# Where a recurrence's carry is computed: TensorE order, and work handed from VectorE to ScalarE and GpSimd

## The chip, the core and the metric

The kernel runs on one core of one Trainium2 chip. The metric is the device time of one execution in microseconds (us). Before the change it is 202.56 us, the median of three executions (202.4, 202.56 and 202.63). The profile was taken in an execution of 202.6 us; from its first to its last instruction it spans 200.9 us, and every start time below counts from that first instruction.

The engines are named as the profile names them: PE is TensorE's matmuls, PEld its weight loads, DVE is VectorE, ACT is ScalarE, POOL is GpSimd, SP is SyncE, which only issues transfers here. A transpose on TensorE is a matmul against the identity and shows as MATMUL.

## What is computed

Two blocks stand one behind the other. The first is a linear recurrence with decay, for 4 batches, 8 heads, 768 steps and heads 48 wide:

```python
for t in range(S):
    cur = np.einsum('bhd,bhe->bhde', u[None] * kt, vt)
    y[:, :, t] = np.einsum('bhd,bhde->bhe', rt, state + cur)
    state = wt[:, :, :, None] * state + np.einsum('bhd,bhe->bhde', kt, vt)
```

Its output, laid out as 4 batches of 768 rows of 384 numbers, is `x` of the second block, a mixture of depths: in each batch the 128 rows with the highest scores go through a two-layer network and are added back, all other rows are passed through.

```python
scores = np.einsum('bsd,d->bs', x, w_gate)
top_idx = np.argpartition(-scores[b], capacity)[:capacity]      # 128 of 768
h = np.maximum(x[b, top_idx] @ w1, 0.0);  ye = h @ w2           # 384 -> 1024 -> 384
out[b, top_idx] = x[b, top_idx] + sigmoid(scores[b, top_idx])[:, None] * ye
```

## The kernel before

The 768 steps of a batch are cut into 6 chunks of 128, so there are 24 chunks, numbered n = 0 to 23 through all batches. Inside a chunk the recurrence becomes matrix products, with k and r scaled by running products of the decay (`K`, `R`); from chunk to chunk a state of 48x48 per head is carried. The last chunk of a batch (n = 5, 11, 17, 23) hands nothing on.

The kernel is written as a loop of turns, and each engine runs its instructions in the order in which the turn lists them. Turn i does the main work of chunk i, prepares chunks i+1 and i+2, and finishes chunk i-1; the network's matmuls are fed in between in small pieces (`fed_in_turn`) as soon as a batch's rows are picked.

```python
def turn(i):
    step(first_left, i + 1)                       # ACT, one column
    ...
    step(own_products, i + 1)                     # POOL  r*k
    step(scores, i)                               # PE    16 matmuls into ps_s
    step(own_values, i)                           # ACT   8 heads, each with a sum
    step(carry, i - 1, work.get(i))               # DVE and POOL: next state
    if i > 0:
        step(scaled, i + 1, "K", "right")         # DVE
    if i >= 0:
        step(own_weights, i + 1)                  # POOL  times u
    ...
    if i < N:
        step(compared, i - 2)                     # PE ps_e, DVE ahead, ACT every
    step(back, i)                                 # PE 4 transposes, ACT copies them to kt
    mix(place="half")
    if not soon:
        step(masked, i)                           # DVE   sc <- ps_s * mask
    step(rows_out, i - 1, soon)                   # PE ps_y, ACT x, POOL x + vo, DMA out
    step(row_scores_soon if soon else row_products, i - 1)   # POOL scr
    step(own_results, i)                          # POOL  vo = v * own
    fed_in_turn(PIECES // 2, 2 if i >= N - 1 else 1)         # PE pieces of the network
    step(inputs_t, i + 1, "R", r_bufs)            # PE 4 transposes
    ...
    step(scaled, i + 1, "R", "left")              # DVE
    step(decays_t, i + 2)                         # PE 4 transposes into ps_w
    mix(place="mid")
    ...
    step(range_check, i + 2)                      # ACT
    ...
    step(outputs_t, i)                            # PE ps_yt, ACT copies it to yt
    step(carry_products, i)                       # PE ps_kv
    fed_in_turn(PIECES - PIECES // 2, 1 if i == N - 1 else 0)
    ...
    step(inputs_t, i + 2, "K", k_bufs)            # PE 4 transposes
    ...
    if not soon:
        step(row_sums, i - 1)                     # ACT
    step(scans, i + 2)                            # DVE, two scans over ps_w
    ...                                           # mix(place="end"), loads
```

The steps that the change or the argument touches, cut:

```python
def own_values(t):
    ...
    for h in range(H):
        nc.scalar.activation(out=rk[:, h, :], in_=rk[:, h, :], func=AF.Copy,
                             accum_out=o[:, h:h + 1])

def outputs_t(t):
    old = state.get(n)
    ps = psS.tile([L, 2, HP, L], FP32, tag="s", name="ps_yt")
    ...   # 16 matmuls of vt and sc, and 16 more of old and R where there is a state
    t["yt"] = lev.tile([L, 2, HP // 2, L], FP32, tag="yt", name="yt")
    nc.scalar.copy(out=t["yt"], in_=ps[:, :, 0:HP // 2, :])

def back(t):
    ...
    ps = dense(psT, "t", lambda j: t["K"][0:DE, j, :], lambda j: 0)
    t["kt"] = kt_bufs[t["n"] % 2]
    nc.scalar.copy(out=t["kt"][:, :, :, 0:D], in_=ps...)

def carry_products(t):
    ...
    t["kv"] = kv = psK.tile([L, HP, D], FP32, tag="kv", name="ps_kv")
    ...   # 16 matmuls of t["kt"] and v

def compared(t):
    ...
    ps = psW.tile([L, L], FP32, tag="w", name="ps_e")
    nc.tensor.transpose(ps, own.to_broadcast([L, L]), ident)
    ...   # DVE: L508 (chunks 1 to 5 of a batch) and L512
    if ci < NCH - 1:
        nc.scalar.copy(out=every[:, lo:hi], in_=ps)
```

Three PSUM pools with one buffer each matter. `psS` holds `ps_s` (the scores) and `ps_yt` (the outputs) in turn, so the scores of the next chunk can only be written when ScalarE has copied `ps_yt` away. `psW` holds `ps_w` (the transposed decays) and `ps_e` (the transposed scores of rows) in turn. `psK` holds `ps_kv`.

Of the kernel before, what the change touches and what calls it, by code (L numbers as in the profile page):

```python
# [10 lines left out]
FP32 = mybir.dt.float32  # L11
# [3 lines left out]
AF = mybir.ActivationFunctionType  # L15
# [3 lines left out]
L = 128  # L19
DP = 64  # L20
NBUF = 4
# [16 lines left out]
def kernel(  # L38
# [40 lines left out]
    nc = tc.nc  # L79
    PSUM = bass.MemoryType.PSUM  # L80

    B, H, S, D = r.shape
# [2 lines left out]
    CAP = moe_capacity  # L85
    NCH = S // L
    HP = H // 2
    NDC = C // L
    NFC = F // L
    NHF = NCH // 2  # L90
    W = HP * L
    DE = DP + D
    assert S % (2 * L) == 0 and C % L == 0 and F % (4 * L) == 0 and H % 2 == 0
    assert HP % 2 == 0 and D <= DP and W <= 512 and C <= 512 and 0 < CAP < S and CAP % L != 1
    assert B * NCH < 256
# [3 lines left out]
    lev = ctx.enter_context(tc.tile_pool(name="lev", bufs=2))  # L99
# [17 lines left out]
    def half(q):  # L117
        return slice(DP * q, DP * q + DP)
# [5 lines left out]
    v_bufs = [consts.tile([L, H, DP], FP32, name=f"v_buf{i}") for i in range(NBUF)]  # L124

    for queue, hs in ((nc.sync, slice(H // 2, H)), (nc.scalar, slice(0, H // 2))):
        queue.dma_start(
            out=w_bufs[0][:, hs, 0:D], in_=w[0, hs, 0:L, :].rearrange("h t d -> t h d")
# [22 lines left out]
    def loads(n):  # L151
        load(v_bufs, v, n - 3)
        load(k_bufs, k, n - 1)
        load(r_bufs, r, n - 1)
        load(w_bufs, w, n)


    for bufs, x, n in (
# [4 lines left out]
    loads(3)  # L163
    w1 = consts.tile([L, NDC, F], FP32)
    w2 = consts.tile([L, NFC, C], FP32)


    weights = [
        (w1[:, i, :], moe_w1[i * L:(i + 1) * L, :]) for i in range(NDC)
    ] + [  # L170
# [25 lines left out]
    for x in (0, 1):  # L196
        for to, src in ((0, DP * x), (D, DP * (1 - x)), (2 * D, D)):
            n = min(D, DE - to)
            nc.gpsimd.tensor_copy(out=turned[:, x, to:to + n], in_=ident[0:DE, src:src + n])
    kt_bufs = [consts.tile([L, HP, 2, DP], FP32, name=f"kt{i}") for i in range(2)]  # L200
    for t in kt_bufs:
# [9 lines left out]
    for t, sign in ((before_f, 1), (after_f, -1)):  # L211
        nc.gpsimd.memset(t, 1.0)
        nc.gpsimd.affine_select(
            out=t, in_=t, pattern=[[sign, L]], base=-1, channel_multiplier=-sign,
# [17 lines left out]

    from_right = consts.tile([L, HP, L], FP32)
    nc.vector.memset(from_right, 0.0)
    nc.vector.memset(from_right[:, :, L - 1], 1.0)
    from_left = [consts.tile([L, HP, L], FP32, name=f"from_left{i}") for i in range(2)]
    for t, fill in zip(from_left, (nc.vector, nc.gpsimd)):
        fill.memset(t, 0.0)
    right_bufs = [consts.tile([L, HP, L], FP32, name=f"right_buf{i}") for i in range(3)]
    for t in right_bufs:  # L240
# [6 lines left out]
    def warm(n):  # L247

        ps = psM.tile([L, 512], FP32, tag="m", name="ps_n")
        for _ in range(n):  # L250
            nc.tensor.matmul(ps, nothing[:, 0:L], nothing, start=True, stop=True)

    def spread(to, row):

        ps = psM.tile([L, C], FP32, tag="m", name="ps_b")
        nc.tensor.matmul(ps, one_row, row, start=True, stop=True)
        nc.scalar.copy(out=to, in_=ps)
# [46 lines left out]
    def check_sums():  # L304

        above = setup.tile([L, 1], FP32)
        nc.vector.tensor_reduce(out=above, in_=guard, axis=AX.X, op=ALU.add)
        below = setup.tile([L, 1], FP32)
        junk = setup.tile([L, N * HP], FP32)
        nc.vector.tensor_scalar(  # L310
            out=junk, in0=alls.rearrange("p n j -> p (n j)"), scalar1=float(LOW ** L),
            scalar2=None, op0=ALU.is_lt, op1=ALU.add, accum_out=below,
        )
        return above, below
# [49 lines left out]
            )  # L364

    def own_results(t):
        t["vo"] = lev.tile([L, H, D], FP32, tag="vo", name="vo", bufs=3)
        nc.gpsimd.tensor_mul(  # L368
            t["vo"], v_bufs[t["n"] % NBUF][:, :, 0:D], t.pop("own").to_broadcast([L, H, D])
        )  # L370

    def scores(t):
        t["ps_s"] = ps = psS.tile([L, 2, HP, L], FP32, tag="s", name="ps_s")
        for j in range(HP):
            for q in (0, 1):
                rows = slice(DP * q, DP * q + D)
                nc.tensor.matmul(  # L377
                    ps[:, q, j, :], t["K"][rows, j, :], t["R"][rows, j, :],
                    start=True, stop=True,
                )  # L380
# [16 lines left out]
    state = {}  # L397
# [60 lines left out]
    def carry_products(t):  # L458
        n = t["n"]
        if chunks[n][1] == NCH - 1:  # L460
            return
        t["kv"] = kv = psK.tile([L, HP, D], FP32, tag="kv", name="ps_kv")
        for j in range(HP):
            for q in (0, 1):
                nc.tensor.matmul(  # L465
                    kv[half(q), j, :], t["kt"][:, j, q, :],
                    v_bufs[n % NBUF][:, 2 * j + q, 0:D], start=True, stop=True,
                )

    def carry(t, nxt):  # L470

        n = t["n"]
        if "kv" not in t:
            return
        kv = t.pop("kv")
        by = nxt["all"].to_broadcast([L, HP, D])
        new = state[n + 1] = lev.tile([L, HP, D], FP32, tag="state", name="state")
        if n in state:
            mid = lev.tile([L, HP, D], FP32, tag="mid", name="mid")
            nc.vector.tensor_add(mid, kv, state[n])  # L480
            nc.gpsimd.tensor_mul(new, mid, by)
        else:
            nc.vector.tensor_mul(new, kv, by)


    groups = [(c0, min(L, CAP - c0)) for c0 in range(0, CAP, L)]
# [32 lines left out]
    def mixture(b):  # L519
# [21 lines left out]
        for gi, (c0, n) in enumerate(groups):  # L541
# [35 lines left out]

            ps = psT.tile([L, NDC, L], FP32, tag="t", name="ps_x")
            for dc in range(NDC):
                nc.tensor.transpose(ps[:, dc, :], xe[:, dc * L:(dc + 1) * L], ident)  # L580
            xeT = mod.tile([L, NDC, L], FP32, name="xeT", bufs=2)
            nc.scalar.copy(out=xeT, in_=ps)  # L582
# [20 lines left out]
    def forward(b, n, idx, xe, xeT, gate, gated):  # L603
# [6 lines left out]
        for f0 in range(0, NFC, 4):  # L610
# [3 lines left out]
            for q in range(4):  # L614
                for dc in range(NDC):
                    nc.tensor.matmul(  # L616
# [33 lines left out]
    def step(f, n, *more):  # L650
        if 0 <= n < N:
            f(work.setdefault(n, dict(n=n)), *more)

    def mix(n=1, place=None):


        while n > 0 and mixing:
            if place is not None and mixing[0][1] not in (None, place):
                return
            try:  # L660
                mixing[0][1] = next(mixing[0][0])
                n -= 1
            except StopIteration:
                mixing.pop(0)
# [16 lines left out]
    def fed_in_turn(n, few):  # L681

        kept = (feed or picked) and (feed or picked)[0][0] == B - 2
        fed(few if kept else n, on=False)
# [6 lines left out]
    def turn(i):  # L691
        soon = i >= N - 1
        step(first_left, i + 1)
        if i < 1:
            step(scaled_aside, i + 1, "K", "right")
        step(own_products, i + 1)
        step(scores, i)
        step(own_values, i)
        step(carry, i - 1, work.get(i))
        if i > 0:  # L700
            step(scaled, i + 1, "K", "right")
        if i >= 0:
            step(own_weights, i + 1)
        if soon:
            step(masked, i)
        if i == N - 1:
            sums.extend(check_sums())
        if i < N:
            step(compared, i - 2)
        step(back, i)  # L710
        mix(place="half")
        if not soon:
            step(masked, i)
        step(rows_out, i - 1, soon)
        step(row_scores_soon if soon else row_products, i - 1)
        step(own_results, i)
        fed_in_turn(PIECES // 2, 2 if i >= N - 1 else 1)
        step(inputs_t, i + 1, "R", r_bufs)
        if i == -1:
            spread(wg_bc, wg_row)  # L720
        step(scaled, i + 1, "R", "left")
        step(decays_t, i + 2)
        mix(place="mid")
        if i == -2:
            warm(2)
        step(range_check, i + 2)
        if i == -1:
            spread(u_bc.rearrange("p h d -> p (h d)"), u_row)
            step(own_weights, i + 1)
        step(outputs_t, i)  # L730
        step(carry_products, i)
        fed_in_turn(PIECES - PIECES // 2, 1 if i == N - 1 else 0)
        if i == N - 1:
            step(compared, i - 1)
        step(inputs_t, i + 2, "K", k_bufs)
        if i == -2:
            warm(1)
        if not soon:
            step(row_sums, i - 1)
        step(scans, i + 2)  # L740
        if 0 <= i - 2 < N - 1 and chunks[i - 2][1] == NCH - 1:
            mixing.append([mixture(chunks[i - 2][0]), "end"])
        mix(place="end")
        if i > -2:
            loads(i + 5)
        if i in WEIGHT_TURNS:
            load_weights(1)
# [93 lines left out]
```

## Time and profile before

| quantity | value |
|---|---|
| median time | 202.56 us |
| span of the profiled execution | 200.9 us |
| busy: PE / PEld | 188.8 us (94%) / 152.9 us (76%) |
| busy: DVE | 160.9 us (80%) |
| busy: ACT | 120.7 us (60%) |
| busy: POOL | 136.6 us (68%) |
| granted TensorE clock | 0.994 |
| `mid` on DVE (L480) | 16 instructions, mean 340 ns |
| first state of a batch on DVE (L483) | 4 instructions, mean 332 ns |
| `state` on POOL (L481) | 16 instructions, mean 506 ns |
| `vo` on POOL (L368) | 24 instructions, mean 830 ns |

The busy times are averages over a program with two very different stages, so they do not say what bounds it; the strip of 40 slices, each 5.02 us wide, does that better. A timeline line gives the start, the length, the engine, the program line, and what was written from what. On VectorE and ScalarE the next instruction often starts before the listed end of the one before, so the cost of an instruction to its engine is read from start to start, not from its length. An idle time stands in square brackets with the instruction that the profile holds to have ended it. The profile names the releaser that came last by its own clock; where the engine named had long been done, another one was meant.

### The profile page before, as it was taken

What the parts mean: (1) busy time and instruction counts of PE and PEld (TensorE: products, weight loads), DVE (VectorE), ACT (ScalarE), POOL (GpSimd) and SP (SyncE); (2) the same over time, 40 slices, a digit from 0 to 9 for tenths busy, and PEclk for the clock granted to TensorE, in tenths of its full rate; (3) what the DMA queues carried; (4) which work ended last, traced back from release to release, by engine and by line L of the source; (5) the groups of instructions that cost most, each with busy time, mean ns of one, the idle gap of its engine ahead of it and who ended that gap; (6) DMA issues with size and microseconds to landing.
All of it is one profiled execution on the core that took longest, in us unless ns stands there. A gap on an engine that the chain in (4) does not pass through costs nothing.

```text
span 200.9 us, 6399 instructions
## 1 busy us (share of the span) xinstructions
PE 188.8 (94%) x2289; PEld 152.9 (76%) x2289; DVE 160.9 (80%) x355; ACT 120.7 (60%) x619; POOL 136.6 (68%) x175
## 2 busy tenths in 40 slices
PE   7899999989799999999999999999999999999970
PEld 2487888767687898897877898897877898866830
DVE  7899999999999968989978888989978884951010
ACT  5586887768754865787456675787456676410300
POOL 8498789886859997669639798668639797121201
PEclk9999999999999999999999999999999999999997
DMA  7999999999989999899894794897764031111101
GB/s 117 163 163 166 178 180 197 223 212 231 197 138 268 251 192 192 209 236 173 175 137 106 136 210 104 128 172 146 139 98 109 17 111 44 39 44 41 39 8 44
DMA packets 105387, 28.81 MB, mean 143 GB/s; under 512 B 100482, under 2 KB 104580, under 8 KB 105348
## 3 DMA queue, kind: packets, MB, share of 16 engines
q1 hardware_dynamic: 104304, 26.65, 74.7%
q0 software_dynamic: 512, 1.57, 2.7%
q8 instruction: 20, 0.33, 0.7%
q14 instruction: 19, 0.16, 0.3%
q10 hardware_dynamic: 532, 0.10, 0.2%
HBM read 22.81 MB, written 5.51 MB: 141 GB/s over the span
## 4 chain that ended last, share of the span: by engine, by line
PE 76%; DVE 9%; ACT 2%; issue 1%; POOL 0%; POOLq 0%; DVEq 0%; ACTq 0%
PE ps_h L616 11%; PE ps_f L628 11%; PE ps_s L377 10%; PE ps_yt L410 10%; PE ps_t L263 8%; PE ps_yt L418 5%; PE ps_kv L465 4%; PE ps_w L263 4%; PE ps_y L270 4%; PE ps_t L270 3%; PE ps_e L506 3%; DVE left L294 2%; DVE right_buf L283 2%; DVE sc L385 1%; DVE R L341 1%
## 5 line engine op out<-in xcount | busy, mean ns | idle before, releaser
L362 ACT ACTIVATE rk<-rk 128x48 f32<-128x48 f32 x192 | 43.7, 230 | 0.1
L435 POOL TENSOR_TENSOR x<-x,vo 128x384 f32<-128x384 f32 x22 | 22.1, 1004 | 22.0 <-ACT x L434 21.9
L362 ACT ACTIVATION_READ_ACCUMULATOR rk<-rk 128x1 f32 x192 | 36.2, 189 | 0.0
L423 ACT COPY yt<-ps_yt 128x512 f32<-128x512 f32 x24 | 14.1, 585 | 29.6 <-PE ps_yt L418 27.3
L294 DVE TENSOR_TENSOR_SCAN left<-ps_w,from_left 128x511 f32<-128x511 f32 x24 | 30.7, 1280 | 0.9
L385 DVE TENSOR_TENSOR sc<-ps_s,before_f 128x1024 f32<-128x1024 f32 x24 | 29.2, 1218 | 0.8 <-PE ps_s L377 0.8
L283 DVE TENSOR_TENSOR_SCAN right_buf<-ps_w,from_right 128x511 f32<-128x511 f32 x24 | 29.1, 1211 | 0.7 <-PE ps_w L263 0.7
L377 PE MATMUL ps_s<-R,K 48*128 48x128 f32 x384 | 27.9, 285 | 0.3 <-ACT yt L423 0.2
L410 PE MATMUL ps_yt<-sc,v_buf 128*64 128x128 f32 x384 | 26.3, 278 | 2.0 <-PE ps_w L263 1.6
L377 PEld LDWEIGHTS ps_s<-R,K 48*128 48x128 f32 x384 | 23.3, 187 | 3.9 <-issue 3.2
L616 PE MATMUL ps_h<-xeT,w 128*128 128x128 f32 x192 | 25.6, 280 | 0.2 <-ACT hid L621 0.2
L410 PEld LDWEIGHTS ps_yt<-sc,v_buf 128*64 128x64 f32 x384 | 20.7, 136 | 6.4 <-PE ps_w L263 2.9
L356 POOL TENSOR_TENSOR rk<-rk,u_bc 128x384 f32<-128x384 f32 x24 | 24.0, 1002 | 1.6 <-DVE alls L289 0.9
L353 POOL TENSOR_TENSOR rk<-r_buf,k_buf 128x384 f32<-128x384 f32 x24 | 24.2, 1007 | 0.0
L616 PEld LDWEIGHTS ps_h<-xeT,w 128*128 128x128 f32 x192 | 22.9, 192 | 1.6 <-ACT xeT L582 0.5
L628 PE MATMUL ps_f<-w,hid 128*128 128x384 f32 x64 | 23.8, 500 | 0.0
L440 POOL TENSOR_TENSOR scr<-x,wg_bc 128x384 f32<-128x384 f32 x22 | 22.0, 1000 | 1.7
L368 POOL TENSOR_TENSOR vo<-v_buf,own 128x384 f32<-128x384 f32 x24 | 19.9, 830 | 1.3 <-ACT rk L362 1.3
L341 DVE TENSOR_TENSOR R<-ps_t,left 128x512 f32<-128x512 f32 x24 | 16.4, 685 | 3.3 <-ACT own L594 1.3
L341 DVE TENSOR_TENSOR K<-ps_t,right_buf 128x512 f32<-128x512 f32 x22 | 15.1, 684 | 4.6 <-PE ps_t L263 4.6
L263 PE MATMUL ps_w<-ident,w_buf 128*128 128x128 f32 x96 | 15.0, 279 | 1.0 <-ACT every L517 0.7
L263 PE MATMUL ps_t<-ident,k_buf 128*128 128x128 f32 x96 | 15.0, 279 | 0.4 <-DMA k_buf<-in_k_dram 0.4
(111 smaller groups left out, 341.8 us busy)
## 6 DMA issues: line engine op xcount, KB each, us to landing
k_buf<-in_k_dram SPq DMA_DIRECT2D x24, 192.0 KB, 5.3
r_buf<-in_r_dram SPq DMA_DIRECT2D x24, 192.0 KB, 5.3
v_buf<-in_v_dram SPq DMA_DIRECT2D x24, 192.0 KB, 4.6
out_dram<-x SPq DMA_DIRECT2D x24, 192.0 KB, 2.4
w_buf<-in_w_dram SPq DMA_DIRECT2D x23, 192.0 KB, 4.7
w<-in_moe_w_dram SPq DMA_DIRECT2D x3, 512.0 KB, 5.9
w<-in_moe_w_dram SPq DMA_DIRECT2D x4, 384.0 KB, 4.9
w_buf<-in_w_dram ACTq DMA_DIRECT2D x1, 96.0 KB, 3.2
```

The source lines that it names most:

```text
L263: nc.tensor.transpose(ps[:, j, :], src(j), ident)
L283: nc.vector.tensor_tensor_scan(out=flat[:, W - 2::-1], data0=wt[:, W - 1:0:-1], data1=from_right.rearrange("p j t -> p (j t)")[:, W - 2::- ...
L294: nc.vector.tensor_tensor_scan(out=left.rearrange("p j t -> p (j t)")[:, 1:W], data0=wt[:, 0:W - 1], data1=start.rearrange("p j t -> p (j ...
L341: nc.vector.tensor_mul(out, t.pop(name + "t"), t.pop(by))
L353: nc.gpsimd.tensor_mul(rk, r_bufs[n % NBUF][:, :, 0:D], k_bufs[n % NBUF][:, :, 0:D])
L356: nc.gpsimd.tensor_mul(t["rk"], t["rk"], u_bc)
L362: nc.scalar.activation(out=rk[:, h, :], in_=rk[:, h, :], func=AF.Copy, accum_out=o[:, h:h + 1])
L377: nc.tensor.matmul(ps[:, q, j, :], t["K"][rows, j, :], t["R"][rows, j, :], start=True, stop=True,)
L385: nc.vector.tensor_mul(t["sc"].rearrange("p q j t -> p (q j) t"), ps.rearrange("p q j t -> p (q j) t"), _heads(before_f, 2 * HP),)
L410: nc.tensor.matmul(ps[half(c), j % 2, j // 2, :], vt[:, 2 * j + q, :], t["sc"][:, q, j, :], start=(j < 2), stop=(old is None), skip_group_ ...
L616: nc.tensor.matmul(ps[:, q, :], w1[:, dc, (f0 + q) * L:(f0 + q + 1) * L], xeT[:, dc, :], start=(dc == 0), stop=(dc == NDC - 1),)
L628: nc.tensor.matmul(ps, hid[:, fc, :], w2[:, fc, :], start=(fc == 0), stop=(fc == NFC - 1))
```

## The change

The change does three things. **First**, in every turn the carry's products (`ps_kv`, TensorE) are put in front of the chunk's outputs (`ps_yt`) instead of behind them. **Second**, for chunks with n < 9 (`AHEAD = S // L + 3`) ScalarE copies `ps_kv` from PSUM to an SBUF tile at once, and the sum with the old state, or for the first chunk of a batch the product that makes the first state, is done by GpSimd from that copy instead of by VectorE from PSUM. **Third**, for chunks 1 to 8 half of the heads of `vo` are computed by ScalarE, one instruction a head with a per-row scale, and GpSimd does the other half, as a balance for what it got. Its purpose is to take work off VectorE in the stretch before the network's matmuls begin.

```diff
--- before.py
+++ after.py
@@ -85,6 +85,8 @@
     CAP = moe_capacity
     NCH = S // L
     HP = H // 2
+
+    AHEAD = S // L + 3
     NDC = C // L
     NFC = F // L
     NHF = NCH // 2
@@ -364,10 +366,17 @@
             )
 
     def own_results(t):
-        t["vo"] = lev.tile([L, H, D], FP32, tag="vo", name="vo", bufs=3)
+        n, own = t["n"], t.pop("own")
+        vo = t["vo"] = lev.tile([L, H, D], FP32, tag="vo", name="vo", bufs=3)
+        vt = v_bufs[n % NBUF]
+        some = H // 2 if 0 < n < AHEAD else H
         nc.gpsimd.tensor_mul(
-            t["vo"], v_bufs[t["n"] % NBUF][:, :, 0:D], t.pop("own").to_broadcast([L, H, D])
-        )
+            vo[:, 0:some, :], vt[:, 0:some, 0:D], own[:, 0:some].to_broadcast([L, some, D])
+        )
+        for h in range(some, H):
+            nc.scalar.activation(
+                out=vo[:, h, :], in_=vt[:, h, 0:D], func=AF.Copy, scale=own[:, h:h + 1]
+            )
 
     def scores(t):
         t["ps_s"] = ps = psS.tile([L, 2, HP, L], FP32, tag="s", name="ps_s")
@@ -466,6 +475,9 @@
                     kv[half(q), j, :], t["kt"][:, j, q, :],
                     v_bufs[n % NBUF][:, 2 * j + q, 0:D], start=True, stop=True,
                 )
+        if n < AHEAD:
+            t["kv"] = lev.tile([L, HP, D], FP32, tag="kvs", name="kvs")
+            nc.scalar.copy(out=t["kv"], in_=kv)
 
     def carry(t, nxt):
 
@@ -475,12 +487,13 @@
         kv = t.pop("kv")
         by = nxt["all"].to_broadcast([L, HP, D])
         new = state[n + 1] = lev.tile([L, HP, D], FP32, tag="state", name="state")
+        aside = n < AHEAD
         if n in state:
             mid = lev.tile([L, HP, D], FP32, tag="mid", name="mid")
-            nc.vector.tensor_add(mid, kv, state[n])
+            (nc.gpsimd if aside else nc.vector).tensor_add(mid, kv, state[n])
             nc.gpsimd.tensor_mul(new, mid, by)
         else:
-            nc.vector.tensor_mul(new, kv, by)
+            (nc.gpsimd if aside else nc.vector).tensor_mul(new, kv, by)
 
 
     groups = [(c0, min(L, CAP - c0)) for c0 in range(0, CAP, L)]
@@ -727,8 +740,8 @@
         if i == -1:
             spread(u_bc.rearrange("p h d -> p (h d)"), u_row)
             step(own_weights, i + 1)
+        step(carry_products, i)
         step(outputs_t, i)
-        step(carry_products, i)
         fed_in_turn(PIECES - PIECES // 2, 1 if i == N - 1 else 0)
         if i == N - 1:
             step(compared, i - 1)
```

## The prediction

> **What bounds the kernel now.** I read the strip of slices first, because the shares of the whole span hide the stages. Its lines for PE and DVE:
>
> ```profile
> PE   7899999989799999999999999999999999999970
> DVE  7899999999999968989978888989978884951010
> ```
>
> From slice 2 to slice 14, roughly 10 to 70 us, VectorE is full. From 70 us on TensorE is full (10.00 of 10 us busy in each window from 70 to 160 us, when the windows are asked for) and VectorE has gaps. The first stage is turns 0 to 9; there the change removes its work. Next I read the timeline of VectorE in turn 4:
>
> ```profile
> 33.34 0.33 DVE L480 TENSOR_TENSOR mid<-ps_kv,state 128x192 f32<-128x192 f32 x1
> 33.59 0.68 DVE L341 TENSOR_TENSOR K<-ps_t,right_buf 128x512 f32<-128x512 f32 x1
> 34.18 0.47 DVE L508 TENSOR_SCALAR_CACHE_REDUCE ahead<-every,score 128x256 bf16<-128x256 f32 x1
> ...
> 34.85 1.22 DVE L385 TENSOR_TENSOR sc<-ps_s,before_f 128x1024 f32<-128x1024 f32 x1
> 35.99 0.68 DVE L341 TENSOR_TENSOR R<-ps_t,left 128x512 f32<-128x512 f32 x1
> 36.58 1.21 DVE L283 TENSOR_TENSOR_SCAN right_buf<-ps_w,from_right 128x511 f32<-128x511 f32 x1
> ```
>
> No line has an idle time in brackets. `mid` is listed with 0.33 us, but `K` starts 0.25 us after it: **0.25 us** is what taking it away can give. The starts of `R` in turns 1 to 9 (18.12, 23.92, 29.88, 35.99, 42.22, 48.33, 54.83, 62.10, 68.07) give turns of 5.80, 5.96, 6.11, 6.23, 6.11, 6.50, 7.27 and 5.97 us. They grow because L508 compares with ever more columns; turn 8 holds the picking of 128 rows.
>
> TensorE has little room in the same stage. Turn 2 to 3:
>
> ```profile
> 25.12 0.65 PE L418 MATMUL ps_yt<-R,state 64*48 64x128 f32 x16
> 25.71 0.67 PE L465 MATMUL ps_kv<-v_buf,kt 128*64 128x48 f32 x16
> 26.31 0.66 PE L263 MATMUL ps_t<-ident,k_buf 128*128 128x128 f32 x4
> 26.90 1.16 PE L377 MATMUL ps_s<-R,K 48*128 48x128 f32 x16
> ...
> 29.36 0.60 PE L263 MATMUL ps_w<-ident,w_buf 128*128 128x128 f32 x4
> 30.07 1.09 PE L410 MATMUL ps_yt<-sc,v_buf 128*64 128x128 f32 x16
> ```
>
> and ScalarE beside it:
>
> ```profile
> 25.90 0.59 ACT L423 COPY yt<-ps_yt 128x512 f32<-128x512 f32 x1 [1.37 <-PE ps_yt L418]
> 26.38 0.53 ACT L445 ACTIVATE scr<-scr 128x384 f32<-128x384 f32 x1
> ...
> 28.57 0.23 ACT L362 ACTIVATE rk<-rk 128x48 f32<-128x48 f32 x1
> 28.87 0.27 ACT L517 COPY every<-ps_e 128x128 f32<-128x128 f32 x1
> 29.03 0.49 ACT L395 COPY kt<-ps_t 128x384 f32<-128x384 f32 x1
> ```
>
> From `ps_yt` complete (25.71) to the next scores (26.90) pass 1.19 us: `ps_kv` and the K transposes, 0.6 us each. The copy of `ps_yt` (25.90 to 26.49) hides under them; the scores need it, as both tiles share the one buffer of `psS`. And `every` and `kt` come some 3 us after that copy started, behind eight sums.
>
> **What the Trainium skill says.** *Trainium Kernel Development and Optimization*, Key Constraints: GpSimd cannot access PSUM. So the sum can only move if ScalarE copies first; the groups of before agree, each POOL group reads SBUF tiles alone. *ScalarE: Activation LUTs*, What ACT_TABLE_LOAD costs: with immediates an ACTIVATE takes 186 ns + 0.833 ns per element, a per-row pointer operand adds about 93 ns, neighbours overlap by about 93 ns. The trace agrees: 384 columns with a pointer bias take 624 ns (L330), without 525 ns (L445). *GPSIMD Engine Reference*, 4.1 Engine selection: two-input arithmetic about twice as slow as on VectorE. Here it is 1.5 times: `state` of 192 columns takes 506 ns, `mid` 340.
>
> **The change part by part.**
>
> *VectorE loses* `mid` or the first state for chunks 0 to 4 and 6 to 8, eight times 0.25 us = **2.0 us**, one in each of turns 1 to 5 and 7 to 9.
>
> *ScalarE gains* in turns 1 to 8 a copy of 192 columns, between the 263 ns of 128 columns and the 480 of 384, about 0.34 long and 0.24 from start to start, and four ACTIVATEs of 48 columns with a pointer: 230 ns (L362) plus about 95 = 0.33, less the 0.09 of overlap = 0.24 each, 0.95 together. These are estimates from those rows and the page. It now does from copy of `yt` to copy of `yt`, by starts: 0.48 + 0.52 + 0.09 + eight sums 1.82 + `every` 0.16 + `kt` 0.37 + `x` 0.37 + range check 0.62 = 4.4 us; with 1.2 more it is 5.6. That fits into turns of 6.
>
> *GpSimd* gains a sum of 192 columns (506 ns, 0.46 to the next) and loses half of `vo` (0.79 to about 0.46). By starts it goes from 5.25 to 5.4 us a turn. The state is then ready about 3 us before `ps_yt` asks for it. No cost.
>
> *TensorE's order* is the part with a price. Behind the outputs only the K transposes (0.59 us) stand before the next scores, while the copy needs 0.19 + 0.59 + 0.04 = 0.82 from the end of the outputs. Turn 5, which has no products, shows the same arrangement already: K transposes at 44.02, scores at 44.84 after an idle 0.17. And the products now wait for `kt`, with the outputs behind them. This closes a **loop**: copy of `yt` starts, `every` ends 3.2 us later, decay transposes 0.44 + 0.05, products 0.59, outputs 1.02 + 0.59, then 0.19 to the next copy. Sum about **6.05 us** a turn (by way of `kt` it is nearly the same). Before, without the products in it, it was 5.5 and did not bind.
>
> *Turn 0* pays first: its outputs start at 12.82, but its `kt` copy runs from 13.00 to 13.46. With products first the outputs end about 1.2 us later; VectorE's mask of turn 1 then starts at 17.0 instead of the 16.74 it could.
>
> Then VectorE's own turns, 0.25 shorter, against the loop of 6.05:
>
> | turn | before | VectorE alone after |
> |---|---|---|
> | 2 | 5.80 | 5.47 |
> | 3 | 5.96 | 5.71 |
> | 4 | 6.11 | 5.86 |
> | 5 | 6.23 | 5.98 |
> | 6 | 6.11 | 6.11 |
> | 7 | 6.50 | 6.25 |
> | 8 | 7.27 | 7.02 |
> | 9 | 5.97 | 5.72 |
>
> (In turn 2, 0.08 of a small wait goes too.) In turns 2 to 4 the loop is longer than VectorE needs, and nothing is gained; stepping through the starts, I get `R` of turn 4 at 36.1, no earlier than before. Turn 5 has no products, so its loop is 5.47 and what the loop had lost is made up. From then VectorE leads again: `R` of turn 6 at 48.3 (0.05 earlier), of turn 7 at 54.5 (0.3), of turn 8 at 61.6 (0.5), of turn 9 at 67.3 (0.8). TensorE ends products and outputs of turn 9 at 69.9 instead of 71.1, since the products filled the wait for the mask. About **1.15 us** are carried into the second stage.
>
> *In the second stage* (turns 10 to 21) TensorE sets the pace, and 0.86 to 1.6 us of network matmuls stand between outputs and scores. They hide the copy; the order costs nothing there, and ScalarE's and GpSimd's work is as before.
>
> *Turn 22* has neither such matmuls nor K transposes there:
>
> ```profile
> 167.52 0.65 PE L418 MATMUL ps_yt<-R,state 64*48 64x128 f32 x16
> 168.10 0.67 PE L465 MATMUL ps_kv<-v_buf,kt 128*64 128x48 f32 x16
> 168.88 1.16 PE L377 MATMUL ps_s<-R,K 48*128 48x128 f32 x16
> ```
>
> The products fill exactly the 0.8 us of the copy. In front of the outputs, which do not wait for a mask there (it is done at 166.21, they start at 166.49), they push the scores of chunk 23 back by about **0.6 us**, and the chain of waits goes on from these scores to the last gather.
>
> Sum: 202.56 - 1.15 + 0.6 = **202.0 us**.
>
> **The rivals.** *VectorE alone decides*: eight times 0.25 comes through, less 0.6 at the end if the last turn pays, about 201.1 (200.5 if it does not). For it: no idle time on VectorE from 17 to 59 us. Against it: the loop through ScalarE. *ScalarE or the loop is dearer than I count*: if the four ACTIVATEs do not overlap, or `kt` comes 0.15 later, turns 2 to 9 run at 6.2 to 6.3, the stage gains nothing, and the 0.6 of turn 22 stays: 203.2. Against it: there is about 0.4 us of slack on ScalarE in the loop. *The new order costs everywhere*: 0.25 in each of the 12 turns of the second stage would add 3 us to my sum and make 205.0; against it stand the network's matmuls between outputs and scores. *Hidden anyway*: if the second stage takes its start from the gathered rows or from transfers, the early gain is lost, 203. Against it: the first network matmuls (71.06) follow TensorE's queue, not a wait.
>
> **Range and chances.** I take 202.0 us, with 201.1 to 203.1 for 8 in 10: the lower end is the first rival, the upper one the second. A gain of 2% would need 4 us, twice what VectorE loses, a loss of 2% the third rival and more. Faster by over 2%: 0.02; within 2%: 0.95; slower by over 2%: 0.03.
>
> **What would show it.** VectorE after: no `mid` or first state up to 66 us, and in turns 2 to 4 idle times in front of `sc`, `ahead` or the first scan, for the loop; none there means the first rival. TensorE: an idle time before `ps_s` in turns 1 to 4 with ScalarE's `yt` as releaser, and before `ps_w` with `every`. Turn 22: scores about 0.8 us after the outputs with nothing between, and from there a shift of 0.6 us. The starts of `R` of turns 4, 6 and 9 tell the early sum. I am wrong if the loop of 6.05 us is not a loop (`every` or `kt` sooner), or if turn 0's loss is never made up.

## The result, and the profile after

The changed kernel takes **201.75 us** (median of four executions) against 202.59 us for the kernel before on the same chip. The ratio is 0.9959, with a 95% interval of 0.9941 to 0.9976: 0.8 us less. The prediction said 202.0. Its mechanisms do not add up to this in the way that it says; the number came out right by luck, and the rest shows how.

The same two lines of the strip, of the kernel after (its slices are 5.00 us):

```profile
PE   7989999999899999999999999999999998999980
DVE  6999899999999978988979888989978983961010
```

VectorE is still busy for 80% or more in each of the slices 2 to 14. The eight sums are gone (347 VectorE instructions instead of 355), yet the first stage does not end earlier. The timeline of VectorE in turn 4, kernel after:

```profile
34.05 0.67 DVE L343 TENSOR_TENSOR K<-ps_t,right_buf 128x512 f32<-128x512 f32 x1
34.63 0.47 DVE L521 TENSOR_SCALAR_CACHE_REDUCE ahead<-every,score 128x256 bf16<-128x256 f32 x1
35.18 0.35 DVE L525 SCALAR_TENSOR_TENSOR ahead<-ps_e,score,after_f 128x128 bf16<-128x128 f32 x1
35.45 1.22 DVE L394 TENSOR_TENSOR sc<-ps_s,before_f 128x1024 f32<-128x1024 f32 x1
36.59 0.68 DVE L343 TENSOR_TENSOR R<-ps_t,left 128x512 f32<-128x512 f32 x1
```

`K` now follows the scan directly. But L525 starts 0.55 us after L521, where the sequence needs 0.40: it waits for `ps_e` (34.82, 0.32 long), which comes behind late scores. `R` of turn 4 starts at 36.59, 0.6 us later than before; 0.2 of that is there at the launch already. TensorE, turns 2 to 3:

```profile
26.37 0.66 PE L427 MATMUL ps_yt<-R,state 64*48 64x128 f32 x16
26.96 0.66 PE L265 MATMUL ps_t<-ident,k_buf 128*128 128x128 f32 x4
27.73 1.16 PE L386 MATMUL ps_s<-R,K 48*128 48x128 f32 x16
...
30.29 0.66 PE L265 MATMUL ps_w<-ident,w_buf 128*128 128x128 f32 x4
30.88 0.67 PE L474 MATMUL ps_kv<-v_buf,kt 128*64 128x48 f32 x16
31.38 1.06 PE L419 MATMUL ps_yt<-sc,v_buf 128*64 128x128 f32 x16
```

and ScalarE beside it:

```profile
27.09 0.59 ACT L432 COPY yt<-ps_yt 128x512 f32<-128x512 f32 x1 [0.39 <-PE ps_yt L427]
27.58 0.53 ACT L454 ACTIVATE scr<-scr 128x384 f32<-128x384 f32 x1
...
29.99 0.25 ACT L530 COPY every<-ps_e 128x128 f32<-128x128 f32 x1
30.13 0.48 ACT L404 COPY kt<-ps_t 128x384 f32<-128x384 f32 x1
...
30.87 1.02 ACT L377 ACTIVATE vo<-v_buf,own 128x48 f32<-128x48 f32 x4
31.79 0.62 ACT L332 ACTIVATE junk<-w_buf,high 128x384 f32<-128x384 f32 x1
32.38 0.31 ACT L480 COPY kvs<-ps_kv 128x192 f32<-128x192 f32 x1
33.09 0.58 ACT L432 COPY yt<-ps_yt 128x512 f32<-128x512 f32 x1 [0.39 <-PE ps_yt L427]
```

The copies of `yt` start at 27.09, 33.09 and 39.08: the turns have locked to **5.99 us**, the loop of the prediction. From the copy of `yt` at 27.09 it goes to `every`, which ends at 30.24, to `ps_w` at 30.29, to the products at 30.88, to the outputs at 31.38, and to the next copy at 33.09. ScalarE waits for 0.39 us of it.

The tail, turn 22 of the kernel after, where nothing stands between outputs and scores any more:

```profile
166.91 0.65 PE L427 MATMUL ps_yt<-R,state 64*48 64x128 f32 x16
168.27 1.16 PE L386 MATMUL ps_s<-R,K 48*128 48x128 f32 x16 [0.70 <-ACT yt L432]
```

**Where the time came from.** The clearest ledger is the start of the scores of each chunk (first `ps_s` line of each turn in TensorE's timeline), as a difference in us from the kernel before. The first line holds what differs at the launch, where the profiles begin up to 0.3 us apart; I take this for chance and do not subtract it. E1 to E8 are the experiments below.

| chunk | before starts at | after | E1 | E2 | E3 | E4 | E5 | E6 | E7 | E8 |
|---|---|---|---|---|---|---|---|---|---|---|
| 0 | 10.01 | +0.21 | -0.04 | +0.28 | -0.01 | -0.04 | +0.07 | +0.18 | +0.02 | +0.11 |
| 1 | 14.88 | +1.13 | +0.89 | +0.29 | +0.91 | +0.89 | +1.00 | +0.19 | +0.03 | +0.12 |
| 5 | 38.97 | +0.75 | +0.68 | -0.36 | +0.54 | +0.52 | +0.63 | -0.46 | -0.62 | -0.53 |
| 8 | 58.31 | -0.45 | -0.03 | -0.88 | -0.66 | -0.68 | -0.57 | -0.97 | -1.13 | -1.05 |
| 10 | 73.03 | +0.01 | +0.39 | -0.76 | -0.24 | -0.07 | -0.53 | -1.07 | -1.67 | -0.46 |
| 17 | 125.33 | -0.67 | -0.30 | -0.76 | -0.93 | -0.76 | -1.21 | -1.75 | -2.44 | +0.58 |
| 22 | 163.26 | -1.08 | -0.71 | -0.76 | -1.34 | -1.16 | -1.61 | -2.16 | -2.91 | +1.32 |
| 23 | 168.88 | -0.61 | -0.24 | -0.77 | -0.88 | -1.16 | -1.61 | -2.17 | -2.91 | +1.31 |

In the column of the kernel after, chunk 10 starts no earlier than before. Nothing is left of the relief of VectorE there. Then 1.09 us come in the second stage, for which the prediction had nothing, and 0.47 go at the tail.

Two things in the profile explain the surprises. First, one of the six picks of turn 8. The line of their group in the kernel after, with the durations min/median/max of 24, and GpSimd's timeline beside it:

```profile
L562 DVE TENSOR_SCALAR pick<-slots,rank x24: 240/249/1041, 58.8 to 178.0; 128x128 bf16<-128x128 bf16 x24
```

```profile
57.70 0.59 POOL L493 TENSOR_TENSOR mid<-kvs,state 128x192 f32<-128x192 f32 x1
58.36 0.51 POOL L494 TENSOR_TENSOR state<-mid,alls 128x192 f32<-128x192 f32 x1
58.82 1.00 POOL L358 TENSOR_TENSOR rk<-rk,u_bc 128x384 f32<-128x384 f32 x1
```

The picks start at 58.84, 0.02 us after GpSimd's product; the first of them takes 1.04 us and ends 0.06 us after that product. Before, the longest pick took 255 ns: GpSimd then stood idle from 57.7 to 60.2, waiting for VectorE's own sum behind the picks. The Trainium skill names such a contention (GPSIMD Engine Reference, 1. Specifications): GpSimd shares its SBUF interfaces with VectorE, in contention with VectorE instructions that use both ports or read two SBUF inputs. That the picks run in such a mode is my reading; the runs show that they are held, and when.

Second, the weight loads of TensorE in turn 13, before and then after:

```profile
97.96 0.85 PEld L410 LDWEIGHTS ps_yt<-sc,v_buf 128*64 128x64 f32 x16 [0.17 <-issue]
98.99 0.40 PEld L418 LDWEIGHTS ps_yt<-R,state 64*48 64x48 f32 x16 [0.17 <-issue]
99.57 0.55 PEld L465 LDWEIGHTS ps_kv<-v_buf,kt 128*64 128x64 f32 x16 [0.18 <-issue]
```

```profile
97.86 0.55 PEld L474 LDWEIGHTS ps_kv<-v_buf,kt 128*64 128x64 f32 x16 [0.17 <-issue]
98.32 0.86 PEld L419 LDWEIGHTS ps_yt<-sc,v_buf 128*64 128x64 f32 x16
99.35 0.40 PEld L427 LDWEIGHTS ps_yt<-R,state 64*48 64x48 f32 x16 [0.17 <-issue]
```

The pair after the names, 128*64 or 64*48, is called the tile here: the rows and columns that the loaded weights take. In these lines there is a gap of 0.17 us, put down to no wait, wherever the tile changes. Products and first half of the outputs have the same pair, 128*64, and as neighbours they have no gap between them. The gap alone is not the measure of the cost: in turn 13 of E8 (below) the loads for `ps_kv` end at 98.08 and those for `ps_w`, with another tile, start at 98.13. What a change costs shows in the times from start to start; TensorE in turn 13, kernel after:

```profile
96.89 0.60 PE L265 MATMUL ps_t<-ident,r_buf 128*128 128x128 f32 x4
97.33 0.60 PE L265 MATMUL ps_w<-ident,w_buf 128*128 128x128 f32 x4
97.86 0.67 PE L474 MATMUL ps_kv<-v_buf,kt 128*64 128x48 f32 x16
98.36 1.06 PE L419 MATMUL ps_yt<-sc,v_buf 128*64 128x128 f32 x16
```

Four transposes take 0.44 us in front of four others of the same tile, though those write another PSUM buffer, and 0.53 in front of the products. The products take 0.50 in front of outputs of their own tile.

### The profile page after: what moved, and what is told of

It reads as the page before. It is cut to its first block, busy times and chain, and to the rows that moved or that the text cites. A ratio compares the mean times of both kernels' runs of the same rounds, so it can differ in the third digit from the quotient of the medians.

```text
span 200.1 us, 6416 instructions
## 1 busy us (share of the span) xinstructions
PE 188.7 (94%) x2289; PEld 152.5 (76%) x2289; DVE 159.8 (80%) x347; ACT 128.8 (64%) x659; POOL 138.4 (69%) x183
## 4 chain that ended last, share of the span: by engine, by line
PE 80%; DVE 7%; ACT 6%; POOL 3%; issue 1%; POOLq 0%; DVEq 0%; ACTq 0%
PE ps_h L629 11%; PE ps_f L641 11%; PE ps_s L386 11%; PE ps_yt L419 9%; PE ps_t L265 8%; PE ps_w L265 5%; PE ps_kv L474 5%; PE ps_yt L427 5%; PE ps_y L272 4%; PE ps_t L272 3%; ACT rk L364 3%; PE ps_e L519 3%; PE ps_n L253 2%; ACT yt L432 2%; DVE left L296 1%
## 5 line engine op out<-in xcount | busy, mean ns | idle before, releaser
L419 PE MATMUL ps_yt<-sc,v_buf 128*64 128x128 f32 x384 | 25.6, 275 | 0.0
L373 POOL TENSOR_TENSOR vo<-v_buf,own 128x384 f32<-128x384 f32 (+1 forms) x24 | 17.3, 722 | 1.4 <-ACT rk L364 1.4
L265 PE MATMUL ps_w<-ident,w_buf 128*128 128x128 f32 x96 | 15.5, 286 | 0.6 <-ACT every L530 0.3
L641 PEld LDWEIGHTS ps_f<-w,hid 128*128 128x128 f32 x64 | 11.1, 190 | 6.0 <-issue 1.1
```

What stands on the lines that cost most here:

```text
L265: nc.tensor.transpose(ps[:, j, :], src(j), ident)
L419: nc.tensor.matmul(ps[half(c), j % 2, j // 2, :], vt[:, 2 * j + q, :], t["sc"][:, q, j, :], start=(j < 2), stop=(old is None), skip_group_ ...
L641: nc.tensor.matmul(ps, hid[:, fc, :], w2[:, fc, :], start=(fc == 0), stop=(fc == NFC - 1))
```

## The experiments

All times are medians. The kernel before was run on the same chip in each group: 202.5 us for E1 to E4, 202.65 for E5 to E8, and 202.59 for the kernel after, so small differences from one group to another are uncertain by 0.1 to 0.2 us. A few executions ran at a lower granted clock (down to 0.975); they weigh in the ratios and hardly in the medians, so a ratio can lie up to 0.003 from that of the medians.

**E1, the order alone.** `AHEAD = 0`: all sums stay on VectorE.

```diff
-    AHEAD = S // L + 3
+    AHEAD = 0
```

> The changed kernel with AHEAD = 0: only the products stand in front of the outputs; VectorE keeps its sums, ScalarE and GpSimd get nothing. Theory (the gain comes from the order on TensorE: products and outputs run next to each other, 0.14 us less in each of nine turns 9, 10, 13 to 16 and 19 to 21 that have both products and a state; the tail of turn 22 gives 0.5 back; the hand-over brings nothing in sum): about 201.7 us, like the changed kernel. Rival of the prediction (the order costs, the relief of VectorE pays): 203 or more.

Measured: **202.33 us**, ratio 0.9983 (0.9971 to 0.9995). This is between the theory (201.7) and the rival (203). A hit on the part of the theory that concerns the second stage, where chunks 10 to 22 gain 1.10 us, and the tail, which gives back 0.47. A miss on the first stage: chunk 10 starts 0.39 us late, and turn 9, which the theory counted among those that gain, gains nothing here. So the order alone costs in the first stage; the hand-over does bring 0.4 to 0.5 us there (chunk 10 of E4 against E1), but that only pays for the loss by the order.

**E2, the hand-over alone.**

```diff
-        step(carry_products, i)
         step(outputs_t, i)
+        step(carry_products, i)
```

> The changed kernel with outputs in front of products again: only the hand-over to ScalarE and GpSimd. Theory: VectorE saves 2.0 us up to turn 9, the loop through ScalarE is 5.4 us and does not bind, but one pick of turn 8 may again stand behind a GpSimd instruction (up to 0.8); no tail loss, no gain per turn in the second stage: 201.0 to 201.6. Rival (VectorE's relief comes through whole): 200.5.

Measured: **201.32 us**, ratio 0.9949 (0.9931 to 0.9967). Chunk 8 starts 0.88 us earlier, although the launch was 0.28 late: the loop of 5.99 is gone, and the copies of `yt` come 5.84 us apart (25.87 and 31.71). From chunk 10 to chunk 23 the difference stands still at -0.76. No gain in the second stage, no loss at the tail: both belong to the order. Again one pick is held (1024 ns), and of the 2.0 us taken from VectorE only 0.76, or about 1.0 with the late launch, reach chunk 10.

**E3, GpSimd kept idle during the picks.** The sum of chunk 7 stays on VectorE.

```diff
-        if n < AHEAD:
+        if n < AHEAD and n != 7:
...
-        aside = n < AHEAD
+        aside = n < AHEAD and n != 7
```

> The changed kernel, but the sum of chunk 7 stays on VectorE, so GpSimd has to wait for it behind the six picks and is idle during them. Theory (a pick of 1041 instead of 249 ns is held by the GpSimd product that runs at the same time): all picks about 250 ns, 0.8 saved, 0.25 given for the sum, and the time falls by about 0.5 to 201.2 us. Rival (the long pick is chance, or the second stage does not take over what turn 8 saves): the time stays at 201.75 or rises by 0.25.

Measured: **201.62 us**, ratio 0.995 (0.9926 to 0.9974). The group of the picks in E3:

```profile
L562 DVE TENSOR_SCALAR pick<-slots,rank x24: 245/249/255, 58.6 to 177.7; 128x128 bf16<-128x128 bf16 x24
```

No pick is held, as the theory said. But the time falls by 0.13 only, not 0.5, and by 0.04 if each is taken against its own runs of the kernel before: the rival had it right, the second stage does not take over what turn 8 saves. Against E4, which began at the same time, chunk 9 gains 0.51, and of that 0.17 is left at chunk 10. What paces the start of the second stage is shown by the chain of waits of the kernel after (start, length, what):

```profile
61.56 0.15 DVE idx L575
61.70 0.28 issue
61.98 1.23 POOL xe L584
63.21 0.04 issue
63.25 1.01 POOL x L444
...
64.34 1.01 POOL scr L449
65.35 0.02 issue
65.37 0.62 ACT scr L454 x2
...
67.88 0.16 ACT every L530
68.04 0.04 issue
68.08 0.66 PE ps_w L265 x4
```

The picked indices release the gather on GpSimd; `x` and `scr` stand behind it in GpSimd's queue; ScalarE's sum of that row waits for `scr`, with the eight sums, `every`, and so `ps_w` behind it. In E3 the indices are ready at 60.73, but GpSimd, which had waited for VectorE's sum, is busy with `state` and the product with u until 61.57 and starts the gather at 61.73, against 61.75 in E4 and 61.98 in the kernel after. So `ps_w` of turn 9 starts only 0.03 us before that of E4 (67.83, 67.86). The rest of the 0.17 is a delay of E4 behind it: there the gathered rows landed 6.6 us after the gather was issued, at 68.35, and their transposes `ps_x` start 0.60 us behind `ps_w` instead of 0.49.

**E4, the old order in turn 22.**

```diff
-        step(carry_products, i)
-        step(outputs_t, i)
+        step(outputs_t if i == N - 2 else carry_products, i)
+        step(carry_products if i == N - 2 else outputs_t, i)
```

> The changed kernel, but in turn 22 the outputs stand in front of the products as before. Theory (the scores of chunk 23 wait bare for the copy of the outputs): they start 0.8 us after the outputs end with the products in between, and the time falls by 0.5 to 201.25 us. Rival (the tail is hidden behind the gather of rows): 201.75 us, no change.

Measured: **201.27 us**, ratio 0.995 (0.9934 to 0.9965). TensorE in turn 22 of E4:

```profile
166.36 0.65 PE L427 MATMUL ps_yt<-R,state 64*48 64x128 f32 x16
166.94 0.67 PE L474 MATMUL ps_kv<-v_buf,kt 128*64 128x48 f32 x16
167.72 1.05 PE L386 MATMUL ps_s<-R,K 48*128 48x128 f32 x14
```

From the end of the outputs to the scores pass 0.78 us, with the products inside. The difference is the same at chunks 22 and 23: the 0.47 are back, and the median is 0.48 us lower than that of the kernel after, as the theory said.

**E5, the picks freed and the gather too.** E4, and in turn 8 GpSimd's product with u stands behind that turn's row products.

```diff
-        if i >= 0:
+        if i >= 0 and i != 8:
             step(own_weights, i + 1)
...
+        if i == 8:
+            step(own_weights, i + 1)
         step(own_results, i)
```

> The changed kernel with the old order in turn 22 (201.27 us by itself) and, in turn 8 alone, GpSimd's product with u behind the row products of that turn instead of ahead of the picks' rows. Theory (that product is the instruction that holds a pick, and the start of the second stage is paced by picks, gather on GpSimd, x, scr, ScalarE's sums, every, ps_w): all picks about 250 ns, the gather starts about 1.0 us earlier than in the kernel with only the old order in turn 22, the scores of chunk 10 by 0.6 to 0.7: about 200.6 us. Rival (TensorE paces the start of the second stage, the picks and the gather do not): 201.1 to 201.3.

Measured: **200.86 us**, ratio 0.9899 (0.9867 to 0.993). The longest pick takes 255 ns. The gather starts at 61.08 instead of 61.75 in E4, 0.67 us sooner, and chunk 10 0.46 us sooner. This is nearer to the theory than to the rival. The start of the second stage follows the gather; 0.26 us of the gain are lost again, since ScalarE's sums wait for the moved product. As picks and gather move together here, E5 alone would not tell them apart; E3, where only the picks were freed, does.

**E6, the new order only in turns 9 to 21.** As E5 otherwise.

```diff
+        late = 9 <= i < N - 2
+        step(carry_products if late else outputs_t, i)
+        step(outputs_t if late else carry_products, i)
```

> As e5, but the products stand in front of the outputs only in turns 9 to 21; before and in turn 22 the old order. Theory (the new order costs in the first stage through the loop of 6.0 us, gains 0.14 in nine turns of the second stage, and the hand-over pays only with the old order): the hand-over alone, 201.3, less 1.2 for the order, less 0.6 for the picks: 199.6 us, the best of all. Rival (the gain per turn hangs on the new order in all turns, or on what the early turns leave behind): 200.6, no better than e5.

Measured: **200.21 us**, ratio 0.9853 (0.9805 to 0.9901). The early turns run as in E2, chunks 10 to 22 gain 1.09 as in the changed kernel, and nothing is lost at the tail. It misses the expected 199.6: in its profile a transfer of `r` came late, GpSimd started 0.35 us later in turn 8, and a pick took 478 ns beside GpSimd's product for `state`, which had moved into its way. The gathered rows came late too: they landed 7.0 us after the issue at 60.34, and `ps_x` starts 0.67 us behind `ps_w` instead of 0.49.

**E7, the products between the two halves of the outputs**, in turns 9 to 21, otherwise as E6. Inside `outputs_t`, behind the matmuls with `sc`:

```diff
+        if late:
+            carry_products(t)
         for j in range(HP if old is not None else 0):
```

> As e6, but in turns 9 to 21 the products stand between the two halves of the outputs: behind those that read sc, in front of those that read the state. Theory (what costs is each change of the tile shape on TensorE, about 0.1 us; products and sc-outputs share a shape, and here too they are neighbours): the same as e6 within 0.2 us. Rival (the gain comes from work that fills a wait for the mask in front of the outputs, which this gives up): 1.2 us more than e6.

Measured: **199.7 us**, ratio 0.9835 (0.9788 to 0.9883), the fastest of all and by the medians 1.5% under the kernel before. Chunks 10 to 22 gain 1.24 us, 0.15 more than in E6, as the theory allows; its rival falls. In the profiles E7 leads E6 by 0.74 us at chunk 23, by the medians by 0.51. Of the 0.74, 0.60 are there at chunk 10 already and have little to do with the edit: 0.16 is the launch, 0.22 the held pick of E6 by chunk 9, and of the 0.22 in turn 9 0.18 is the late `ps_x` of E6.

**E8, the products in front of the decay transposes**, in turns 9 to 21, otherwise as E6.

```diff
+        late = 9 <= i < N - 2
+        if late:
+            step(carry_products, i)
         step(decays_t, i + 2)
```

> As e6, but in turns 9 to 21 the products stand one place earlier still, in front of the decay transposes, so that they are no longer neighbours of the outputs. Theory (changes of tile shape): two more changes than e6 in each of eleven turns, 0.2 us each: 1.8 to 2.2 us more than e6. Rival (products ahead of the outputs help by filling waits): the same as e6 or less.

Measured: **203.43 us**, ratio 1.0042 (1.0013 to 1.007), 3.2 us more than E6. TensorE in turn 13 of E8:

```profile
97.53 0.67 PE L474 MATMUL ps_kv<-v_buf,kt 128*64 128x48 f32 x16
98.13 0.66 PE L265 MATMUL ps_w<-ident,w_buf 128*128 128x128 f32 x4
98.72 1.09 PE L419 MATMUL ps_yt<-sc,v_buf 128*64 128x128 f32 x16
99.74 0.65 PE L427 MATMUL ps_yt<-R,state 64*48 64x128 f32 x16
```

The products take 0.60 from start to start instead of 0.50 in the kernel after, the decay transposes 0.59 instead of 0.53. The rival, that products in front help by filling waits, falls. Counted in changes of tile from the R transposes to what follows:

| kernel, turn 13 | sequence | changes | turn against before |
|---|---|---|---|
| after, E6 | R, w / kv, yt / state part / next | 3 | -0.13 |
| before | R, w / yt / state part / kv / next | 4 | 0 |
| E8 | R / kv / w / yt / state part / next | 5 | +0.15 |

Turn 12 has no state part: before and after have two changes each there, and the turn does not change (0.02); E8 has four, and it is 0.31 longer. So one change costs about **0.14 us**, and the new order saves one in each of eight turns between chunks 10 and 22, 1.1 us. The Trainium skill has a sentence for it (TensorEngine Tiling (Array Packing), Key Properties): "Changing tiling mode (not just tile) drains the TensorE". No run here shows a drain as such, only gaps of 0.17 us in front of weight loads, at many of the changes, and the cost of 0.14.

From chunk 10 to 22 this gives E8 eight turns of 0.15 and two of 0.31, 1.8 us more than before; measured are 1.78. My expectation for E8 took a change at 0.1 us and was too low: against E6, E8 loses 3.18 us between chunks 9 and 22, and eleven turns with two changes more each, at 0.14, make 3.1. Another 0.30 are there at chunk 9 in this profile, of another cause: GpSimd waited 1.22 us for a late `r`, and two picks were held by what this moved beside them (591 and 500 ns).

## Why the prediction was right in its number and wrong in its sum

*VectorE loses 2.0 us*: right as a sum of work, eight instructions and 0.25 each. That it does not come through was right as well, and the first rival, in which it does, is refuted by the column of the kernel after.

*ScalarE's new work*: right. Four ACTIVATEs take 0.92 us from start to start (predicted 0.95), the copy 0.31 long (0.34), and ScalarE still waits 0.39 us in the loop (predicted 0.4).

*GpSimd*: the sum takes 0.59, and up to 0.68 to the next start, not 0.46. The state is still ready in time. But "No cost" was wrong: what the new work does to a pick stands below.

*The loop*: right in kind, 5.99 instead of 6.05 us, though not term by term. The terms as printed add up to 6.08. Measured from the lines above, the decay transposes take 0.59 instead of 0.44, the products 0.50 instead of 0.59, as they now have the outputs as neighbours, and from the start of the outputs to the copy pass 1.71 instead of 1.80.

*Turn 0*: right for the mask of turn 1, which starts at 16.97 in E4 (predicted 17.0). Chunk 1 starts 0.9 us late there, and `R` behind the mask at 18.38, 0.26 later than before, which the prediction did not have.

*"About 1.15 us are carried into the second stage"*: this step failed. Chunk 10 starts 0.01 us later than before, or 0.07 us earlier in E4. The signs that the prediction named tell where it went: `R` of turns 4, 6 and 9 starts at 36.36, 48.47 and 68.22 in E4, where it had 36.1, 48.3 and 67.3. So 0.2 to 0.3 us were lost by turn 4, and 0.7 more between `R` of turn 7 (54.70, where it had 54.5) and of turn 8 (62.52, where it had 61.6), which is where the picks stand. The scores of chunk 8, ahead of them, still start 0.68 us early. Two things that I had not looked for take the gain away: the hand-over puts GpSimd to work during the picks of turn 8, and one of them is held 0.8 us; and the second stage begins at the pace of indices, gather, `x`, `scr`, sums, not of VectorE's scans or TensorE's queue. The rival "hidden anyway" came near: the second stage takes its start from the gather, mostly through GpSimd's queue behind it, and in E4 and E6, to judge by the landing times, by another 0.1 to 0.2 us through the gathered rows themselves. Two waits of the kernel before, in turn 9, were there to be read:

```profile
65.22 0.52 ACT L445 ACTIVATE scr<-scr 128x384 f32<-128x384 f32 x1 [0.55 <-POOL scr L440]
67.94 0.66 PE L263 MATMUL ps_w<-ident,w_buf 128*128 128x128 f32 x4 [0.23 <-ACT every L517]
```

VectorE's last scan ahead of that turn ended at 65.64, about 0.1 us before ScalarE, held back by `scr`, came to write its column of the same tile at 65.75: a faster VectorE alone had next to nothing to gain there.

*"The order costs nothing there"*: this failed too, to the other side. It gains 0.14 us in each of eight turns, 1.1 us. I had counted what stands between two instructions and taken the length of each as fixed.

*Turn 22*: right in kind; 0.47 instead of 0.6, since the products in front save their change of tile there too. E4 takes it back.

So the sum of the changed kernel is 0.0 to chunk 10, -1.1 to chunk 22, +0.5 to chunk 23: -0.6, and -0.8 in the medians. The 0.2 between them lies behind the scores of chunk 23: from there to the end pass 32.0 us before and 31.8 after, and 31.7 to 32.0 in the other runs, so no cause is read into it. The two errors, 1.15 too much at chunk 10 and 1.1 too little behind it, were of nearly equal size and cancelled: that was luck. In the prediction the hand-over earned the gain and the order cost; in the runs the order earns it from turn 10 on and costs before, and the hand-over earns 0.4 to 0.6 us on top of E1 (by chunk 10, and by the medians).

## What to carry to other kernels

An instruction moved to another engine also occupies that engine at a time when it used to wait; look at what runs beside the wait that disappears, for here it was a pick that VectorE could not finish beside GpSimd. On TensorE, put groups of matmuls with the same tile next to each other: the length of a group depends on its neighbour. A change of order that pays in one stage should be tried stage by stage: the order of the outputs and products was worth 1.1 us in turns 10 to 21, and cost in turns 0 to 8 and in turn 22.

## What the hardware showed that I had not expected

A VectorE pick of 128 bf16 columns took 249 ns alone and up to 1041 ns beside one GpSimd product of 1.00 us. The held picks of the kernel after, E2, E4, E6 and E8 (1041, 1024, 1043, 478, 591 and 500 ns) ended 0.04 to 0.06 us after a GpSimd product did, whatever the time they had waited. The scans and the mask kept their lengths through all this (1.21, 1.28 and 1.22 us in the median, before and after). A change of the tile on TensorE cost about 0.14 us for fp32 groups of 4 to 16 matmuls, with tiles of 128*128, 128*64 and 64*48 in turn.
